# Six instead of three value blocks a layer moved onto chosen load engines, three of them fed by the Pool queue

## The chip, the core and the metric

The kernel runs on one core of a Trainium2 chip. The metric is the device time of one launch in microseconds (us), lower is better; the median of three runs before the change is 2574.92 us (2574.52 to 2575.61). All arithmetic is in float32.

## The reference

Two tokens (batch 2, one position, width 512) go twice through the same pair of layers: grouped attention over a cache of 32768 keys with 32 query heads on 8 key heads, and a gated feed-forward layer with a rectified gate.

```python
x = x + attention(layernorm(x), k_cache, v_cache, wq, wo)   # k, v: 2 x 8 x 32768 x 128
x = x + feed_forward(layernorm(x), W_gate, W_up, W_down)    # 512 -> 1792 -> 512
x = x + attention(layernorm(x), k_cache, v_cache, wq, wo)   # the same weights and caches again
x = x + feed_forward(layernorm(x), W_gate, W_up, W_down)
# attention: p = softmax(q k^T / sqrt(128)); out = (p v) reshaped @ wo
# feed_forward: gate = x W_gate; up = x W_up; (gate * (gate > 0) * up) @ W_down
```

The two caches hold 268 MB each and are read once a layer, but for a small part that the kernel keeps on the chip between its layers.

## The kernel before

A layer is 16 turns (`NG`), one for each pair of key head and batch entry. A turn needs the 32768 keys and the 32768 values of its pair, laid out by the host as 64 blocks of 128 partitions x 512 numbers (2 KB a partition). Half of them, 32 blocks (64 KB a partition, 8 MB), is one load. Eight blocks are a page.

SBUF holds one long tile, `arena`: three slots of 64 KB a partition, used in turn (`by_use`, `used`), and 29 KB beside them for small tiles (`ring`). Every big load is issued by SyncE (queue SP) in program order and waits there until its slot has been read out by TensorE. So the order of the loads is that of the code: in step `i` of a layer's loop come both halves of the keys of turn `i` (`keys`), then both halves of the values of turn `i-1` (`values`), and on TensorE the products with them in the same order. `k_tile` makes the scores of a page, `soft_max` the exponentials, `soft_tail` the transposed probabilities (VectorE, 32x32 blocks), `v_tile` adds the products with a page of values up in `acc`, `evacuate` scales `acc` into SBUF, `head_out` and `project` bring it through `wo`.

A load over 128 partitions gives each of the 16 load engines (the DMA engines) 8 partitions, that is 16 KB of each block. One group of blocks is treated apart. In turn `SIDE_TURN` the last `SIDE` = 3 blocks of page `SIDE_PAGE` are left out of the ordinary value load. The host has cut the 96 keys a row group that they hold into other rows (`side_blocks`, array `side`): two sets of 20 partitions, each with 20 KB a partition, whose source has 5 outer rows, so that 5 engines carry them. SP issues these two loads at the end of `values(SIDE_TURN)` and they take a slot of their own. Their products follow at once (`v_side`, 10 products over 64 partitions), with keys that `side_keys` made in `soft_tail` of that turn: three transposes of windows of the probabilities `p`, one memset on GpSimd, and one product with the mask `side_rows` that clears the unused rows.

Weights of the other stages go through the small tiles in pieces. At the end of layer 0 the next layer's first keys and part of its first values stay on the chip.

Of the kernel before, what the change touches and what calls it, by code (L numbers as in the profile page):

```python
# [46 lines left out]
C_SAME, C_MEAN, C_SEL, C_PAIR, C_SIDE, C_ONE, C_MHALF, C_END = 0, 128, 160, 192, 224, 225, 226, 228  # L47


@with_exitstack  # L50
def attention_reglu_decode(ctx: ExitStack, tc: tile.TileContext, x, k, v, wq, wo, wgu, wd, consts, side, out):
# [12 lines left out]
    def ring(at, width):  # L64
        if at < 0:
            assert at * KB + width <= 0 or (spill[0] + 1) * SLOT == RING
            at += (spill[0] + 1) * SLOT - RING
        at = int((RING + at) * KB)
        return arena[:, at : at + width]

    def slot(s, at=0, width=SLOT * KB):
        at = int((s * SLOT + at) * KB)
        return arena[:, at : at + width]

    def load(t, src):
        nc.sync.dma_start(t, src)
        return t
# [52 lines left out]
    selh = sel[:, :16]  # L130
    col = sel[:, :NB]
    pair = cst[:, C_PAIR : C_PAIR + 32]
    side_rows = cst[:, C_SIDE : C_SIDE + 1]
# [140 lines left out]

    def side_keys(p):
        W = SIDE_CHUNKS * 32
        t = ring(SIDE_KEYS_AT, 2 * W)
        at = SIDE_PAGE // 2 % 2 * D + (SIDE_PAGE % 2 * 8 + 8 - SIDE) * 32  # L280

        def windows(rows):
            return bass.AP(rows.tensor, rows.offset + at, [rows.ap[0], [SIDE_ROWS, SIDE_CHUNKS], [1, 32]])

        def chunks(rows):
            return rows.rearrange("p (k r) -> p k r", r=32)

        nc.gpsimd.memset(t[64:, W:], 0.0)
        nc.vector.transpose(chunks(t[:, :W]), windows(p))
        for c in (0, 32):  # L290
            nc.vector.transpose(chunks(t[c : c + 32, W:]), windows(p[64 + c : 96 + c]))
        nc.vector.tensor_scalar_mul(t, t, side_rows[:, 0:1])
        return t

    def v_side(L, n):
        s = by_use[0]
        vt = slot(s, 0, 2 * SIDE_CHUNKS * D)
        for c in range(2):
            load(vt[32 * c : 32 * c + SIDE_ROWS], side[L, c, :, : 8 * SIDE_CHUNKS * D].rearrange("e (r f) -> e r f", r=4))
        used(s)  # L300
        t, J = side_of.pop(n), SIDE_PAGE // 4
        for k in range(2 * SIDE_CHUNKS):
            nc.tensor.matmul(
                acc[32 * (k % 4) : 32 * (k % 4) + 16, :],
                t[:, 32 * k + 16 * J : 32 * k + 16 * J + 16],
                vt[:, k * D : (k + 1) * D],
                start=False, stop=k >= 2 * SIDE_CHUNKS - 4,
            )

    def v_tile(n, j, vt, first, last, blocks):  # L310
# [87 lines left out]
    for L in range(NLAYER):  # L398
# [3 lines left out]
        def keys(i):  # L402
            n = seq[i]
            if i < NG - 1:
                place_queries(i + 1, seq[i + 1])
            if L and i == 0:
                loads = list(kept_k)
                kept_k.clear()
            elif L and i == 1:
                f, g = key_slots  # L410
                loads = cuts(k, n, [(f, 0, 0, 8), (f, 16, 8, 16), (f, 32, 16, 32), (g, 0, 32, 48), (g, 32, 48, 64)])
            elif i == NG - 1:
                f, g = key_slots[:] = by_use[:2]
                loads = cuts(k, n, [(f, 0, 0, 32), (g, 0, 32, 48), (g, 32, 48, 64)])
            else:
                loads = whole(k, n)
            if not last and i == NG - 1:
                loads = list(loads)
                kept_k.extend(loads)
            for lo, _, t in by_page(loads):  # L420
                j = lo // 8
                k_tile(L, i, n, j, t)
                if L and i == 0:
                    yield
                if j == 1 and i >= 1:
                    soft_tail(L, i - 1, seq[i - 1])
                if j == 2 and i >= 2:
                    head_out(L, seq[i - 2])
                    if i % 2 == 1:
                        project((i - 3) // 2, load(ring(WO_AT, REP * D), wo[seq[i - 2] // NB]), False)  # L430
                    if i == NG - 1:
                        gather()

        def values(i, soft):
            n = seq[i]
            if i == NG - 1:
                if last:
# [108 lines left out]
```

## Time and profile before

| | |
|---|---|
| median of 3 runs (lowest to highest) | 2574.92 us (2574.52 to 2575.61) |
| the profiled execution's own time | 2574.12 us |
| its span, first to last instruction | 2572.3 us |
| TensorE busy with products | 51% of the span |
| VectorE busy | 6% |
| GpSimd busy | 6.7 us in 11 instructions |
| moved by DMA | 1105.95 MB in 29429 packets, mean 430 GB/s |
| share of the SP queue's packets of 16 engines' span | 99.7% |
| granted TensorE clock, mean | 0.75 |

The table is from the first three parts of the page and from the times. Busy times are sums over an engine's instructions; the share of a DMA queue is the time of its packets over 16 engines for the whole span, so 100% would mean that no load engine ever stood still. A view that cuts the span into stretches gives the same share for each of them: with 16 engines, one that stands still takes 0.06 off.

### The profile page before, as it was taken

Reading aid. Unit: us, or ns where it says so; the run is one execution under the profiler, and the core shown is the slowest. Engines: PE = TensorE matmul, PEld = TensorE weight load, DVE = VectorE, ACT = ScalarE, POOL = GpSimd, SP = SyncE. Lnnn points to the kernel's source line nnn. Section 1 sums busy time; section 2 is a strip of 40 time slices with the busy share of each in tenths; the row PEclk is TensorE's granted clock in tenths of the full one; section 3 lists DMA queues with packets and bytes.
Section 4 is the critical chain, followed back from the end, with each engine's and each line's share of the span. In section 5 each row is a group of like instructions: output and inputs, shape, how many; then the busy total and the mean of one; then the engine's idle time right before and its main releaser. Section 6 shows DMA issues by size and latency. Waiting matters only on the chain.

```text
span 2572.3 us, 19897 instructions
## 1 busy us (share of the span) xinstructions
PE 1304.3 (51%) x9452; PEld 342.7 (13%) x9452; DVE 153.0 (6%) x367; ACT 41.3 (2%) x69; POOL 6.7 (0%) x11
## 2 busy tenths in 40 slices
PE   2544454455445544555675554455445544554555
PEld 0111111111111111111121111111111111111112
DVE  0000000000000000000011000000000000000001
ACT  0000000000000000000000000000000000000000
POOL 0000000000000000000000000000000000000000
PEclk9777777777767777777887777777776777777788
DMA  9999999999999999999999999999999999999998
GB/s 425 430 432 438 431 432 431 435 429 437 427 435 436 426 437 430 436 431 421 422 412 434 436 430 433 435 432 434 430 438 426 436 434 430 437 428 433 431 435 376
DMA packets 29429, 1105.95 MB, mean 430 GB/s; under 512 B 3276, under 2 KB 3540, under 8 KB 6740
## 3 DMA queue, kind: packets, MB, share of 16 engines
q1 hardware_dynamic: 29188, 1104.56, 99.7%
q8 instruction: 74, 1.21, 0.2%
q10 hardware_dynamic: 160, 0.12, 0.0%
q14 instruction: 7, 0.06, 0.0%
HBM read 1104.60 MB, written 0.07 MB: 429 GB/s over the span
## 4 chain that ended last, share of the span: by engine, by line
DMA 67%; PE 24%; another core or an unknown queue 9%; DVE 0%; issue 0%; SPq 0%; ACTq 0%; POOL 0%; POOLq 0%; DVEq 0%
DMA arena<-k 46%; DMA arena<-v 16%; PE sc_odd L241 9%; PE sums L317 6%; PE sc_even L241 5%; DMA arena<-wo 2%; DMA cst<-consts 1%; DMA arena<-wd 1%; PE po L337 1%; PE sc_odd L210 1%; PE sums L241 1%; PE sums L348 1%; DMA arena<-wgu 1%; DMA arena<-wq 0%
## 5 line engine op out<-in xcount | busy, mean ns | idle before, releaser
L317 PE MATMUL sums<-arena 128*16 128x512 f32 (+1 forms) x4116 | 582.3, 717 | 600.7 <-DMA arena<-v 600.7
L241 PE MATMUL sc_odd<-arena,qz 128*32 128x512 f32 x2048 | 302.5, 745 | 293.6 <-DMA arena<-k 293.6
L241 PE MATMUL sc_even<-arena,qz 128*32 128x512 f32 x1920 | 277.5, 731 | 286.0 <-DMA arena<-k 286.0
L317 PEld LDWEIGHTS sums<-arena 128*16 128x16 f32 x4116 | 119.6, 109 | 1014.0 <-issue 519.6
L241 PEld LDWEIGHTS sc_odd<-arena,qz 128*32 128x32 f32 x2048 | 71.6, 133 | 504.6 <-DMA arena<-k 321.2
L241 PEld LDWEIGHTS sc_even<-arena,qz 128*32 128x32 f32 x1920 | 64.7, 131 | 473.2 <-DMA arena<-k 312.6
L331 DVE TENSOR_SCALAR arena<-sums,stat 128x512 f32<-128x512 f32 (+1 forms) x38 | 24.8, 665 | 779.4 <-PE sums L317 725.1
L266 DVE STREAM_TRANSPOSE arena<-arena 128x512 f32<-128x512 f32 x64 | 41.5, 687 | 2.5 <-ACT arena L259 2.5
L250 DVE TENSOR_REDUCE stat<-sc_odd 128x1 f32<-128x1024 f32 x16 | 19.6, 1225 | 339.7 <-PE sc_odd L241 339.7
L259 ACT ACTIVATE arena<-sc_odd,stat 128x1024 f32<-128x1024 f32 x16 | 17.8, 1114 | 1177.2 <-DVE stat L256 1177.2
L250 DVE TENSOR_REDUCE stat<-sc_even 128x1 f32<-128x1024 f32 x15 | 18.4, 1225 | 299.8 <-PE sc_even L241 299.8
L337 PE MATMUL po<-cst,arena 128*128 128x4 f32 x256 | 34.8, 259 | 1.8 <-DVE arena L331 1.8
L337 PEld LDWEIGHTS po<-cst,arena 128*128 128x128 f32 x256 | 32.0, 195 | 26.1 <-issue 23.5
L259 ACT ACTIVATE arena<-sc_even,stat 128x1024 f32<-128x1024 f32 x15 | 16.7, 1114 | 1069.9 <-DVE stat L256 1069.9
L272 DVE RECIPROCAL stat<-sm 128x1 f32<-128x1 f32 x32 | 5.3, 166 | 414.0 <-PE sm L270 414.0
L256 DVE TENSOR_REDUCE stat<-mp 128x1 f32<-128x32 f32 x32 | 6.1, 192 | 360.3 <-PE mp L254 360.3
L372 PE MATMUL sc_odd<-arena 128*32 128x224 f32 x256 | 19.7, 452 | 14.8 <-DMA arena<-wgu 13.5
L348 PE MATMUL sums<-arena,oT 128*2 128x512 f32 x112 | 15.4, 623 | 16.3 <-DMA arena<-wo 13.0
L210 PE MATMUL sc_odd<-arena 128*32 128x512 f32 x128 | 20.5, 733 | 5.6 <-DMA arena<-wq 3.1
L254 PEld LDWEIGHTS mp<-arena,cst 128*128 128x128 f32 x64 | 13.1, 257 | 52.4 <-issue 50.7
L162 PE MATMUL meana<-cst,stat 128*128 128x32 f32 x4 | 1.0, 342 | 35.5 <-DMA cst<-consts 35.0
L254 PE MATMUL mp<-arena,cst 128*128 128x32 f32 x64 | 17.0, 354 | 3.5 <-DVE arena L253 3.5
(70 smaller groups left out, 152.5 us busy)
## 6 DMA issues: line engine op xcount, KB each, us to landing
arena<-v SPq DMA_DIRECT2D x17, 2048.0 KB, 15.7
arena<-k SPq DMA_DIRECT2D x7, 4096.0 KB, 20.9
arena<-wo SPq DMA_DIRECT2D x16, 1024.0 KB, 50.9
arena<-v SPq DMA_DIRECT2D x2, 7424.0 KB
arena<-v SPq DMA_DIRECT2D x2, 4096.0 KB
arena<-wgu SPq DMA_DIRECT2D x8, 896.0 KB, 13.6
arena<-wgu SPq DMA_DIRECT2D x4, 1792.0 KB
arena<-wq SPq DMA_DIRECT2D x6, 1024.0 KB, 8.6
```

The costliest lines, as they stand in the source:

```text
L210: nc.tensor.matmul(qp[32 * c : 32 * c + 32, B, :], xT[:, kt, :], t[:, e * D : (e + 1) * D], start=kt == 0, stop=kt == KT - 1)
L241: nc.tensor.matmul(sc_of[n][32 * c : 32 * c + 32, B, :], qz[:, i % 2, 28 - 4 * j : 60 - 4 * j], kt[:, ch * D : (ch + 1) * D], start=j == 0 ...
L250: nc.vector.tensor_reduce(m1, sc_of[n], AX.XY, ALU.max)
L254: nc.tensor.matmul(mp[:, :32], same, mt, start=True, stop=True)
L256: nc.vector.tensor_reduce(nm, mp[:, :32], AX.X, ALU.max, negate=True)
L259: nc.scalar.activation(p, sc_of[n].rearrange("p a b -> p (a b)"), AF.Exp, bias=nm[:, 0:1], scale=1.0, accum_out=rs)
L266: nc.vector.transpose(pT[:, B * D : (B + 1) * D], p[:, B * D : (B + 1) * D])
L317: nc.tensor.matmul(acc[32 * c : 32 * c + 16, e * w : (e + 1) * w], pT[:, B, m, 16 * J : 16 * J + 16], vt[:, at * D + e * w : at * D + (e + ...
L331: nc.vector.tensor_scalar_mul(acs[:, at : at + w], acc[:, at : at + w], linv[:, 0:1])
L337: nc.tensor.matmul(po[:, :REP], acs[:, t * P : (t + 1) * P], selh[:, 4 * t : 4 * t + 4], start=t == 0, stop=t == 3)
L348: nc.tensor.matmul(op[32 * u : 32 * u + NB, :], oT[:, u, :], w[:, u * D : (u + 1) * D], start=pair_at == 0, stop=pair_at == HKV - 2)
L372: nc.tensor.matmul(gu[32 * j : 32 * j + 32, s, :], xT[:, at + e, :], t[:, f : f + HF], start=at + e == 0 and s == 0, stop=at + e == KT - 1 ...
```

## The change

`SIDE` goes from 3 to 6 blocks, `SIDE_TURN` from turn 13 to turn 11 of 16, and the rows of these blocks are cut anew:

- One SP load (`side`) brings 20 partitions of 48 KB, 5 outer rows, 12 packets of 16 KB for each of 5 engines; before it was two loads of 20 KB a partition, 8 packets of 20 KB for each of the five.
- Three loads of 4 partitions of 48 KB each (`alone`, to partitions 28, 64 and 92) are issued by GpSimd on the Pool queue. Their two access patterns have 4 and 3 outer rows. Ahead of the first and of the third go small loads of 4-byte elements (`turn_by`, into `turned`, which nothing reads), with 7 and 6 outer rows. The code counts on two things that the trace before cannot show, since its Pool queue carries nothing: that a load with 4 and 3 outer rows stays on one engine, and that the Pool queue deals its loads out to the engines in rotation. Then the small loads turn it on by 7 and by 6, and the three loads fall to engines 7, 8 and 15.
- The products (`v_side`, now 24 over 96 partitions) and the `evacuate` of that turn move from the end of `values(SIDE_TURN)` into `keys(SIDE_TURN + 2)`, after the second page of its first half. Until then the side blocks hold their slot.
- `side_keys` makes two key tiles `t` and `u` with eight transposes and four memsets, masks both and adds them.
[...]

```diff
-SCRATCH = 64
+SCRATCH = 512
-SIDE_TURN = NG - 3
-SIDE_PAGE, SIDE = 3, 3
-SIDE_WAYS, SIDE_ROWS, SIDE_CHUNKS, SIDE_GAP = 5, 20, 5, 64
+SIDE_TURN = NG - 5
+SIDE_PAGE, SIDE = 3, 6
+SIDE_WAYS, SIDE_ROWS, SIDE_CHUNKS, SIDE_GAP = 5, 20, 24, 64
+SIDE_END, ALONE, TURNED = 96, (28, 64, 92), (7, 0, 6)
...
     def side_keys(p):
...
-        nc.gpsimd.memset(t[64:, W:], 0.0)
-        nc.vector.transpose(chunks(t[:, :W]), windows(p))
-        for c in (0, 32):
-            nc.vector.transpose(chunks(t[c : c + 32, W:]), windows(p[64 + c : 96 + c]))
+        for g, c in enumerate((0, 1, 3)):
+            nc.vector.transpose(chunks(t, 0, 8 * g, 8), windows(c, 0, 20, 8))
+            nc.vector.transpose(chunks(u, 0, 8 * g, 8), windows(c, 132, 4, 8))
+        nc.vector.transpose(chunks(t, 2, 0, 24), windows(2, 0, 4, 24))
+        nc.vector.transpose(chunks(u, 2, 0, 24), windows(2, 68, 4, 24))
+        for c in (1, 3):
+            nc.gpsimd.memset(t[32 * c : 32 * c + 32], 0.0)
+            nc.gpsimd.memset(u[32 * c : 32 * c + 32], 0.0)
         nc.vector.tensor_scalar_mul(t, t, side_rows[:, 0:1])
+        nc.vector.scalar_tensor_tensor(t, u, side_rows[:, 1:2], t, ALU.mult, ALU.add)
...
-    def v_side(L, n):
+    def turn_by(n):
+        if n:
+            few = consts[: 5 * n, :1].rearrange("(e r) f -> e r f", r=5)[:, :4]
+            nc.gpsimd.dma_start(turned[: 4 * n, steps[0] : steps[0] + 1], few)
+        steps[0] += 1
+    def load_side(L, n):
         s = by_use[0]
-        vt = slot(s, 0, 2 * SIDE_CHUNKS * D)
-        for c in range(2):
-            load(vt[32 * c : 32 * c + SIDE_ROWS], side[L, c, :, : 8 * SIDE_CHUNKS * D].rearrange("e (r f) -> e r f", r=4))
+        vt = side_at[n] = slot(s, 0, 3 * SIDE_THIRD).rearrange("p (a f) -> p a f", a=3)[:, :, : SIDE_CHUNKS * D // 3]
+        load(vt[:SIDE_ROWS], side[L, :, : 4 * SIDE_CHUNKS * D])
+        part = 4 * SIDE_CHUNKS * D // 3
+        for e, (row, step) in enumerate(zip(ALONE, TURNED)):
+            turn_by(step)
+            nc.gpsimd.dma_start(vt[row : row + 4], alone[L, e, :, :part])
         used(s)
+    def v_side(n):
...
+                t[:SIDE_END, 32 * k + 16 * J : 32 * k + 16 * J + 16],
+                vt[:SIDE_END, k // 8, k % 8 * D : (k % 8 + 1) * D],
...
                 k_tile(L, i, n, j, t)
+                if j == 1 and i == SIDE_TURN + 2:
+                    v_side(seq[SIDE_TURN])
+                    evacuate(seq[SIDE_TURN], False)
...
             if i == SIDE_TURN:
-                v_side(L, n)
-            evacuate(n, i == NG - 1)
+                load_side(L, n)
+            else:
+                evacuate(n, i == NG - 1)
```

TensorE in layer 0 before, around the side products: L317 are products with values, L241 with keys, L303 those with the side blocks, `sm` belongs to `soft_tail`.

```order
L317 MATMUL sums<-arena 16x512 x8
L254 MATMUL mp_14_2285<-arena,cst 128x32
L317 MATMUL sums<-arena 16x512 x53
L303 MATMUL sums<-arena 16x512 x10
L241 MATMUL sc_odd<-arena,qz 32x512 x16
L270 MATMUL sm_14_2378<-stat,cst 128x1
```

The same engine after; L342, L244 and L328 are now the products with values, keys and side blocks, L362 is `head_out`.

```order
L257 MATMUL mp_12_1988<-arena,cst 128x32
L342 MATMUL sums<-arena 16x512 x16
L342 MATMUL sums<-arena 16x256 x4
L342 MATMUL sums<-arena 16x512 x32
L244 MATMUL sc_odd<-arena,qz 32x512 x16
L328 MATMUL sums<-arena 16x512 x24
L273 MATMUL sm_12_2097<-stat,cst 128x1
L244 MATMUL sc_odd<-arena,qz 32x512 x8
L362 MATMUL po_11_2108<-cst,arena 128x4 x4
```

The side products stood right behind the values of their turn; now they stand behind two pages of the next loaded keys, two turns earlier in the layer.

SyncE's queue in layer 0 after, around the side load, with what each load waits for (PE: its slot has been read; DMAHW and DMASW: earlier loads of the SP and ACT queues and of the Pool queue).

```order
L78 DMA arena<-v 128x13312 [waits DMAHW6_49,PE_49]
L78 DMA arena<-v 128x16384 [waits DMAHW7_49,PE_49]
L78 DMA arena<-side 20x3x4096 [waits DMAHW3_49,DMAHW0_49,PE_49]
L78 DMA arena<-k 128x16384 [waits DMAHW1_49,PE_49]
L78 DMA arena<-wo 128x2048
L78 DMA arena<-k 128x16384 [waits DMAHW2_49,PE_49]
L78 DMA arena<-v 128x16384 [waits DMASW4_49,DMASW2_49,DMAHW3_49,DMASW1_49,PE_49]
```

The last row is the next load into the slot that the side blocks hold: between the side load and it stand two loads of keys and `wo`, and its wait for TensorE is now the wait for the 24 side products.

GpSimd in layer 0 after, from the last of its four memsets on (L310 the turning loads, L322 the single-engine loads, L221 belongs to the queries of layer 1).

```order
L300 MEMSET arena 32x768
L310 DMA turned<-consts 28x1x1
L322 DMA arena<-alone 4x3x4096 [waits DMAHW0_49,PE_49]
L322 DMA arena<-alone 4x3x4096
L310 DMA turned<-consts 24x1x1
L322 DMA arena<-alone 4x3x4096
L221 TENSOR_TENSOR stat<-stat,cst 128x2 [waits DVE_49,Pool_49]
```

GpSimd, which issued no load before, now issues five in each layer; the first of the big ones waits until TensorE has read the slot out, and until layer 1 nothing but the other loads is queued behind it.

More of the change, by code (lines that the diff above doesn't have):

```diff
@@ L41, with attention_reglu_decode @@
 ENDING = (3, 2, 2, 1)
-SIDE_TURN = NG - 3
-SIDE_PAGE, SIDE = 3, 3
-SIDE_WAYS, SIDE_ROWS, SIDE_CHUNKS, SIDE_GAP = 5, 20, 5, 64
-C_SAME, C_MEAN, C_SEL, C_PAIR, C_SIDE, C_ONE, C_MHALF, C_END = 0, 128, 160, 192, 224, 225, 226, 228
+SIDE_TURN = NG - 5
+SIDE_PAGE, SIDE = 3, 6
+SIDE_WAYS, SIDE_ROWS, SIDE_CHUNKS, SIDE_GAP = 5, 20, 24, 64
+SIDE_END, ALONE, TURNED = 96, (28, 64, 92), (7, 0, 6)
+SIDE_THIRD = SIDE_CHUNKS * D // 3 + 16
+C_SAME, C_MEAN, C_SEL, C_PAIR, C_SIDE, C_ONE, C_MHALF, C_END = 0, 128, 160, 192, 224, 226, 227, 229
 @with_exitstack
-def attention_reglu_decode(ctx: ExitStack, tc: tile.TileContext, x, k, v, wq, wo, wgu, wd, consts, side, out):
+def attention_reglu_decode(ctx: ExitStack, tc: tile.TileContext, x, k, v, wq, wo, wgu, wd, consts, side, alone, out):
     nc = tc.nc
@@ L132, in attention_reglu_decode @@
     pair = cst[:, C_PAIR : C_PAIR + 32]
-    side_rows = cst[:, C_SIDE : C_SIDE + 1]
+    side_rows = cst[:, C_SIDE : C_SIDE + 2]
+    turned = sb.tile([4 * max(TURNED), NLAYER * len(TURNED)], F32, name="turned")
     mhalf = cst[:, C_MHALF : C_MHALF + NB]
@@ L278, in side_keys @@
         W = SIDE_CHUNKS * 32
-        t = ring(SIDE_KEYS_AT, 2 * W)
+        t, u = (ring(SIDE_KEYS_AT + e * W / KB, W) for e in range(2))
         at = SIDE_PAGE // 2 % 2 * D + (SIDE_PAGE % 2 * 8 + 8 - SIDE) * 32
[L282 to L286, printed above, removed]
-        nc.gpsimd.memset(t[64:, W:], 0.0)
-        nc.vector.transpose(chunks(t[:, :W]), windows(p))
@@ L290, in side_keys, with windows, chunks @@
-        for c in (0, 32):
-            nc.vector.transpose(chunks(t[c : c + 32, W:]), windows(p[64 + c : 96 + c]))
+        def windows(c, start, step, n):
+            rows = p[32 * c : 32 * c + 32]
+            return bass.AP(rows.tensor, rows.offset + at + start, [rows.ap[0], [step, n], [1, 32]])
+        def chunks(t, c, lo, n):
+            return t[32 * c : 32 * c + 32, 32 * lo : 32 * (lo + n)].rearrange("p (k r) -> p k r", r=32)
+        for g, c in enumerate((0, 1, 3)):
+            nc.vector.transpose(chunks(t, 0, 8 * g, 8), windows(c, 0, 20, 8))
+            nc.vector.transpose(chunks(u, 0, 8 * g, 8), windows(c, 132, 4, 8))
@@ L300, in v_side @@
+    steps, side_at = [0], {}
+    def load_side(L, n):
+        s = by_use[0]
+        vt = side_at[n] = slot(s, 0, 3 * SIDE_THIRD).rearrange("p (a f) -> p a f", a=3)[:, :, : SIDE_CHUNKS * D // 3]
[4 more added lines that the diff above has]
+            nc.gpsimd.dma_start(vt[row : row + 4], alone[L, e, :, :part])
         used(s)
-        t, J = side_of.pop(n), SIDE_PAGE // 4
@@ L302, in v_side @@
-        for k in range(2 * SIDE_CHUNKS):
+    def v_side(n):
+        vt, t, J = side_at.pop(n), side_of.pop(n), SIDE_PAGE // 4
+        for k in range(SIDE_CHUNKS):
             nc.tensor.matmul(
                 acc[32 * (k % 4) : 32 * (k % 4) + 16, :],
-                t[:, 32 * k + 16 * J : 32 * k + 16 * J + 16],
-                vt[:, k * D : (k + 1) * D],
-                start=False, stop=k >= 2 * SIDE_CHUNKS - 4,
+                t[:SIDE_END, 32 * k + 16 * J : 32 * k + 16 * J + 16],
+                vt[:SIDE_END, k // 8, k % 8 * D : (k % 8 + 1) * D],
+                start=False, stop=k >= SIDE_CHUNKS - 4,
@@ L501 @@
     cst[:, C_PAIR : C_PAIR + 32] = np.equal.outer(rows // 4, np.arange(32))
-    cst[:, C_SIDE] = (rows < 64) & (rows % 32 < SIDE_ROWS)
+    cst[:, C_SIDE] = (rows < SIDE_ROWS) | (rows // 4 == 16)
+    cst[:, C_SIDE + 1] = (rows // 4 == 7) | (rows // 4 == 23)
     cst[:, C_ONE] = 1.0 / D
@@ L512, in side_blocks @@
     def side_blocks(v):
-        W = 2 * SIDE_CHUNKS * D
-        sets = np.zeros((NLAYER, 2, SIDE_WAYS, 4 * W + SIDE_GAP), np.float32)
+        W = SIDE_CHUNKS * D
+        side = np.zeros((NLAYER, SIDE_WAYS, 4 * W + SIDE_GAP), np.float32)
+        alone = np.zeros((NLAYER, len(ALONE), 3, 4 * W // 3 + SIDE_GAP), np.float32)
         for L in range(NLAYER):
@@ L518, in side_blocks @@
             keys = v[n, SIDE_PAGE // HALF, :, hi - SIDE * D : hi].reshape(4, 32, SIDE, D).transpose(0, 2, 1, 3)
-            rows = np.zeros((4, SIDE_CHUNKS * SIDE_ROWS, D), np.float32)
-            rows[:, : 32 * SIDE] = keys.reshape(4, 32 * SIDE, D)
-            rows = rows.reshape(2, 2, SIDE_CHUNKS, SIDE_ROWS, D).transpose(1, 3, 0, 2, 4)
-            sets[L, ..., : 4 * W] = rows.reshape(2, SIDE_WAYS, 4 * W)
-        return sets
+            keys = keys.reshape(4, 32 * SIDE, D)
+            low = keys[[0, 1, 3]]
+            side[L, :, : 4 * W] = low[:, :160].reshape(3, 8, SIDE_ROWS, D).transpose(2, 0, 1, 3).reshape(SIDE_WAYS, 4 * W)
+            fours = (low[:, 160:], keys[2, :96], keys[2, 96:])
+            for e, rows in enumerate(fours):
+                rows = rows.reshape(SIDE_CHUNKS, 4, D).transpose(1, 0, 2)
+                alone[L, e, :, : 4 * W // 3] = rows.reshape(3, 4 * W // 3)
+        return side, alone
     wq = con(a["A_wq"].reshape(D, 2, HKV * REP // 2, 4, 32).transpose(0, 1, 3, 2, 4)).reshape(D, -1)
@@ L536 @@
     }
-    arrays["side"] = side_blocks(arrays["v"])
+    arrays["side"], arrays["alone"] = side_blocks(arrays["v"])
     nc = bacc.Bacc("TRN2", target_bir_lowering=False, num_devices=1, dynamic_dma_scratch_size=SCRATCH)
```

## Prediction

> **What bounds the kernel now.** I read the page from its top, then the chain that ended last, then the span cut into stretches at the end of each layer, then single groups for prices. From the page:
>
> ```profile
> span 2572.3 us, 19897 instructions
> PE 1304.3 (51%) x9452; PEld 342.7 (13%) x9452; DVE 153.0 (6%) x367; ACT 41.3 (2%) x69; POOL 6.7 (0%) x11
> DMA packets 29429, 1105.95 MB, mean 430 GB/s; under 512 B 3276, under 2 KB 3540, under 8 KB 6740
> q1 hardware_dynamic: 29188, 1104.56, 99.7%
> q8 instruction: 74, 1.21, 0.2%
> q10 hardware_dynamic: 160, 0.12, 0.0%
> DMA 67%; PE 24%; another core or an unknown queue 9%; DVE 0%; issue 0%; SPq 0%; ACTq 0%; POOL 0%; POOLq 0%; DVEq 0%
> ```
>
> TensorE works half of the span, the load engines all of it, and the chain is mostly DMA. So the kernel lasts as long as its latest load engine needs; what the others do beside it is free. The question is how uneven the 16 are. In the stretches (the last two columns are the DMA share and GB/s) it can be counted, 0.0625 for each engine:
>
> ```profile
> 1219.00:1224.00 5.00, 5.00 (x47) 1.33 (x43) 1.66 (x3) 1.21 (x2) 0.00 (x0) 1.00 0.86 354
> 2563.00:2564.00 1.00, 1.00 (x24) 1.00 (x20) 0.90 (x5) 0.00 (x0) 0.00 (x0) 0.50 0.79 330
> 2566.50:2567.00 0.50, 0.00 (x0) 0.00 (x0) 0.00 (x0) 0.00 (x0) 0.00 (x0) 1.00 0.50 197
> 2567.00:2567.50 0.50, 0.34 (x13) 0.37 (x17) 0.00 (x0) 0.00 (x0) 0.00 (x0) 1.00 0.36 143
> 2568.00:2568.50 0.50, 0.40 (x19) 0.16 (x11) 0.00 (x0) 0.00 (x0) 0.00 (x0) 1.00 0.24 74
> 2568.50:2569.00 0.50, 0.50 (x19) 0.24 (x11) 0.00 (x0) 0.00 (x0) 0.00 (x0) 1.00 0.00 0
> 2561.20:2566.60 5.40, 4.35 (x74) 2.96 (x66) 1.50 (x7) 0.36 (x1) 0.00 (x0) 0.68 0.82 336
> ```
>
> At the end of the launch three engines are done by 2561.2 (0.79 to 0.82 is 13 of 16), eight by 2566.7, ten by 2567.2, and about four work until 2568.5. At the end of layer 0 (1219 to 1224) two to three stand still again. So three engines have 5 to 7 us to spare in each layer while the latest set the pace. That the pace is theirs in both places shows in the chain, here at the end of layer 0 and at the end of the launch (start, length, what):
>
> ```profile
> 1228.92 17.57 DMA arena<-v
> 1269.87 18.50 DMA arena<-wo
> 1288.51 1.12 PE sums L181 x32
> 2543.06 25.24 DMA arena<-wd
> 2568.34 1.11 PE tot L181 x24
> 2569.48 0.35 DVE x L185
> ```
>
> Why they are uneven: the 74 instruction packets took 0.2% of 16 x 2572.3 us, or 82 us, 1.1 us each (0.8 to 1.4 by the rounding). Dealt evenly they would cost each engine 5 us. The records of single landings, which no view lists, show that they are not: before the side loads of each layer eight engines land within 1.5 us of the first, the other eight 4.7 to 6.7 us behind it, growing in steps of 1.5 us at the times of those packets. The side loads of before charge five of the early eight; three early ones are left, those that stand still above.
>
> **The change, part by part.** *Bytes.* A full load takes 19.35 us, the distance of two waits for values that ended with a landing:
>
> ```profile
> 1069.61 3.61 PE L317 MATMUL sums<-arena 128*16 128x512 f32 x16 [9.37 <-DMA arena<-v]
> 1088.96 9.39 PE L317 MATMUL sums<-arena 128*16 128x512 f32 x64 [10.11 <-DMA arena<-v]
> ```
>
> It is 32 blocks, so a block (16 KB an engine) costs each engine 0.605 us. Per layer, against a plain load of all blocks, before and after:
>
> - the eight late engines: 3 blocks less (-1.81 us), now 6 less (-3.63): they gain 1.81 us;
> - engines 0 to 4: 160 KB side rows less 48 KB, now 192 less 96: they gain 16 KB, 0.6 us;
> - the three idle ones: 48 KB less, now 96 more: they lose 9 blocks, 5.45 us.
>
> The three then end at 2561.2 + 5.45 = 2566.7, ahead of today's last 2568.4. If one of the last four is of the five, a layer gains 0.6 us, if none is, up to 1.7 (2568.4 less 2566.7). By the landing records the last is a late engine, 7.9 us behind the first, and the latest of the five is 7.2 behind; the change makes that 7.9 - 1.8 = 6.1 and 7.2 - 0.6 = 6.6, so the gain is 7.9 - 6.6 = 1.3 us. At the end of layer 0 the same records have 2.5 us for the last late engine, 1.8 for the last of the five: 1.8 - 0.6 = 1.2, again 1.3 us. That layer's chain is DMA up to 1288.37, so it counts too. I take 1.3 for each layer, between the ends 0.6 and 1.7.
>
> *The slot held longer.* Issue to landing of a big load and the products of the side blocks:
>
> ```profile
> arena<-v SPq DMA_DIRECT2D x55, 48.3
> 1028.44 5.51 PE L241 MATMUL sc_odd<-arena,qz 128*32 128x512 f32 x32 [10.99 <-DMA arena<-k]
> 1173.57 2.74 PE L303 MATMUL sums<-arena 128*16 128x512 f32 x20
> SPq L76 <- PE sums L303: 3.4, 3, 2.1
> ```
>
> A load is issued 48.3 us ahead of its landing and needs 19.35 itself: 29 us of other loads lie ahead of it. The slot of the side blocks is now free only after two pages of keys (5.51 us) and 24 side products (48 instructions of 2.74/20 us, 6.6 us), 12.4 us with the issue, behind a landing, and ahead of the next load into it lies only one half of keys, 19.35 us. The latest engine has 7 us to spare, one that leads it by 4 us (the widest spread left after the side loads) still 3. The wait of SP costs nothing; behind it on SP stand only loads that land later. TensorE itself has pauses of 9 to 11 us ahead of each half (the waits above), which cover 14 more products, some 4 us. `head_out` of the turn now follows its `evacuate` closely, with a page of keys between.
>
> *VectorE and GpSimd.*
>
> ```profile
> L289 DVE STREAM_TRANSPOSE arena<-arena 128x160 f32<-128x160 f32 x1 | 0.3, 303 | 0.0
> L291 DVE STREAM_TRANSPOSE arena<-arena 32x160 f32<-32x160 f32 x2 | 0.7, 336 | 0.0
> L266 DVE STREAM_TRANSPOSE arena<-arena 128x512 f32<-128x512 f32 x4 | 2.6, 687 | 0.0
> L292 DVE TENSOR_SCALAR arena<-arena,cst 128x320 f32<-128x320 f32 x1 | 0.4, 386 | 0.1
> L272 DVE RECIPROCAL stat<-sm 128x1 f32<-128x1 f32 x1 | 0.2, 168 | 13.3 <-PE sm L270 13.3
> L138 POOL MEMSET arena<- x1: 4364/4364/4364, 1.0 to 1.0; 128x5120 f32 x1
> ```
>
> From 160 to 512 columns a transpose grows by 0.35 us, 1.0 ns a column: six of 256 columns at 0.43 us and two of 768 at 0.94, and two passes over 768 columns at about 0.85 each, 6.2 us instead of 1.4. They fall into the 13.3 us in which VectorE waits for `sm`. Four memsets at 768/5120 of 4.36 us are 2.6 us on an idle GpSimd. The mask's column, `SCRATCH` and the 52 elements of 4 bytes of the turning loads a layer I set at 0: the ACT queue's 160 packets show 0.0% of the engines.
>
> *Packets of the Pool queue.* No trace here has one. Between SP's packets of 64 KB there go 12 of 16 KB on each of the three engines. Below, they cost their bytes, 0.605 us each, as in the sum; above, as much as an instruction packet of the same 16 KB, 1.1 us. [...] They are issued when a slot comes free, with some 29 us of SP's loads still ahead, and the three engines lead at that time: no one waits for them.
>
> **Sum.** 2 x 1.3 = 2.6 us: 2574.1 of the profiled execution becomes 2571.5. The median lies 0.8 above it, so 2574.9 becomes 2572.3. That is 0.1%, half of the 0.2% (5.1 us) that a measurement of this kernel can tell from no change. A bound from above: the stretches from 2561.2 to 2568.5 hold about 2.3 us of idle time per engine, so perfect balance would bring no more than that there, and about as much in layer 0.
>
> **Rivals.** *No gain at all:* one of the five is the last in both layers and a step of 1.5 us falls on it, or the turn order shifts the instruction packets. Two times 0.6 us or less: 2573.7 to 2576. For it: the five end within 0.7 us of the last.
>
> *Slower, the Pool packets cost more than their bytes.* Place: the three engines. With 1.1 us a packet, 12 x 0.5 = 6 us more, they end at 2566.7 + 6 = 2572.7, 4.3 behind today's last, and nothing later in the layer evens that out: +8.6 us, 2583.5. It decides from 1.7 us on, 0.14 us a packet; from 0.36 a packet it would be measurable. For it: the instruction row; against it: the ACT row.
>
> *Slower, the bytes go to other engines.* If the three loads fall to late engines, those lose 9 blocks against now, 5.45 us: an average one, done at 2567.2, ends at 2572.7, +4.3 a layer, 2583.5. If each load deals its 4 partitions to engines 0 to 3, these get 240 KB instead of 112, +4.8 us: 7.2 + 4.8 = 12.0 against 7.9, +4.1 a layer, 2583.1. [...]
>
> *Engines run dry at the held slot:* the side products would have to end 7 us later than worked out, then 1 us more for each further one. I see nothing that would do it.
>
> *Clearly faster:* over 5.1 us would need more than perfect balance gives.
>
> **How the numbers follow.** The forecast (2571 to 2574) has 0.57, no gain 0.20, dear Pool packets 0.08, other engines 0.09, a dry slot 0.02, clearly faster 0.04. The first two lie within 0.2%, and so would the cheap half of the dear packets: same 0.78, slower 0.18, faster 0.04. The range takes in the first two and the low ends of the slower ones: 2569.5 to 2579.5, which leaves out the 0.17 of full price above and a little below.
>
> **What would show it.** In the last 10 us the DMA share stays near 1.0 until about 2565 and then falls within 2 us, instead of standing at 0.8 for 5 us. Near the end of layer 0 the dip to 0.86 is gone or shallower. The wait for `wd` ends 2 to 3 us earlier. A Pool queue appears with 36 packets of 16 KB a layer, about 0.6 us each. If the dear packets were right, three engines would work alone at the end, share 0.19; if the bytes went elsewhere, 1 to 4 engines would, with others still idle early. VectorE's waits for `sm` and `po` should not grow, nor SP's for the side products beyond some us.

## The result and the profile after

The changed kernel takes 2597.39 us, median of four runs (2594.80 to 2598.69), beside 2574.72 for the kernel before, also in four runs (2574.33 to 2575.61). The ratio is 1.0086, 95% interval 1.0069 to 1.0104: some 22.5 us slower, where 2.6 us less had been forecast, and far above the range. The profiled execution took 2594.80 us. From its page:

```profile
span 2593.0 us, 20044 instructions
PE 1306.7 (50%) x9504; PEld 346.3 (13%) x9504; DVE 162.6 (6%) x379; ACT 41.3 (2%) x69; POOL 18.5 (1%) x27
GB/s 422 435 436 425 437 429 435 433 428 435 435 433 433 424 439 427 363 423 429 425 420 434 435 434 430 431 434 426 440 430 432 436 433 428 433 357 436 428 440 373
q1 hardware_dynamic: 29218, 1103.31, 98.8%
q0 software_dynamic: 1376, 1.19, 0.1%
L328 PE MATMUL sums<-arena 96*16 96x512 f32 x96 | 15.2, 799 | 31.3 <-DMA arena<-alone 16.3
```

The same GB/s line of the kernel before:

```profile
GB/s 425 430 432 438 431 432 431 435 429 437 427 435 436 426 437 430 436 431 421 422 412 434 436 430 433 435 432 434 430 438 426 436 434 430 437 428 433 431 435 376
```

TensorE's work and the bytes are nearly what they were; the SP queue's share fell from 99.7% to 98.8%, and 0.9% of 2593 us is 23 us, about the whole loss. It is lost at two places: of the 40 slices two that were full before, the 17th (363 GB/s) and the 36th (357), are the side stretches of the two layers. The last line of the first block says what for: TensorE stood still ahead of the side products, for a single-engine load (`alone`).

Here is TensorE around the side products of layer 0 (start, length, engine, operation, and in brackets the idle time ahead and what ended it):

```profile
1027.18 4.99 PE L244 MATMUL sc_odd<-arena,qz 128*32 128x512 f32 x32 [12.62 <-DMA arena<-k]
1048.43 8.01 PE L328 MATMUL sums<-arena 96*16 96x512 f32 x48 [16.26 <-DMA arena<-alone]
1079.41 3.61 PE L342 MATMUL sums<-arena 128*16 128x512 f32 x16 [9.95 <-DMA arena<-v]
```

The two pages of keys are done at 1032.2, the side rows are there at 1048.4. The other engines in the same stretch, GpSimd and then SyncE:

```profile
979.27 1.33 POOL L322 DMA_DIRECT2D arena<-alone  x2 [934.48 <-PE sc_even L244]
980.59 0.59 POOL L310 DMA_DIRECT2D turned<-consts  x1
1018.88 0.66 POOL L322 DMA_DIRECT2D arena<-alone  x1 [37.70 <-issue]
```

```profile
978.98 0.94 SPq L78 DMA_DIRECT2D arena<-side  x1
993.88 0.35 SPq L78 DMA_DIRECT2D arena<-k  x1
994.28 0.42 SPq L78 DMA_DIRECT2D arena<-wo  x1
1014.62 0.33 SPq L78 DMA_DIRECT2D arena<-k  x1
1056.49 6.49 SPq L78 DMA_DIRECT2D arena<-v  x2
```

SP's next load into the slot goes out at 1056.49, the moment the side products end; what it had issued before (the last at 1014.62) is used up by then. The chain of waits runs the same way, `alone`, side products, next values:

```profile
1018.88 29.30 DMA arena<-alone
1048.18 0.24 issue
1048.43 8.01 PE sums L328 x48
1056.43 0.06 PE sm L273
1056.49 22.87 DMA arena<-v
```

And the stretches show the load engines running dry (last two columns: DMA share and GB/s):

```profile
1040.00:1044.00 4.00, 0.00 (x0) 0.00 (x0) 0.00 (x0) 0.00 (x0) 0.00 (x0) 0.50 1.01 434
1044.00:1048.00 4.00, 0.00 (x0) 0.00 (x0) 0.00 (x0) 0.00 (x0) 0.00 (x0) 0.50 0.41 172
1048.00:1052.00 4.00, 3.57 (x20) 0.93 (x24) 0.00 (x0) 0.00 (x0) 0.00 (x0) 0.50 0.00 0
1052.00:1058.00 6.00, 6.00 (x52) 1.56 (x42) 1.50 (x3) 0.00 (x0) 0.00 (x0) 0.85 0.42 142
1058.00:1062.00 4.00, 3.75 (x39) 1.61 (x35) 0.68 (x3) 0.00 (x0) 0.00 (x0) 1.00 0.72 311
```

The missing shares are 2.4 + 4.0 + 3.5 + 1.1 = 11 us per engine. Layer 1 has the same kind of hole at 2308 to 2326, 10 us by the same sum. The two holes make 21 us, and the profiled execution is 20.7 us longer than that of before (2594.8 against 2574.1).

Why the loads are late is in the records of single packets, which no view lists. In layer 0 the Pool queue's packets of 16 KB took 0.61 us each, as forecast. But as long as SP's packets have 64 KB, each comes 3.03 us behind the one before on its engine: one packet of SP (2.42 us) stands between the two. And a load on one engine is not on one engine alone: of the 1376 packets 72 are the data (16 KB), the other 1304 have 4 or 16 bytes. Each of the three loads puts 12 small packets on each engine that it gives no data, and one more on all 16; a turning load puts 2 on each. The first turning load of a layer waits for nothing and has passed long before (its 32 packets at 49 to 53 us in layer 0). So in the side stretch an engine passes 13 + 13 + 2 + 13 = 41 packets of that queue, and if each waits for one of SP's, that is 41 packets of SP. The data packets by their starts:

```
first load     984.1 ... 1015.0   12 packets, 3.03 us apart but for one pair
second load   1013.2 ... 1027.3   the last nine 0.9 us apart, beside the 8-KB packets of wo
third load    1028.3 ... 1047.1   six 3.03 us apart, the last six with nothing of SP beside them
```

### The profile page after: what moved, and what is told of

Its sections match the earlier page's. It is cut to its first block, busy times and chain, and to the rows that moved or that the text cites. A ratio compares the mean times of both kernels' runs of the same rounds, so it can differ in the third digit from the quotient of the medians.

```text
span 2593.0 us, 20044 instructions
## 1 busy us (share of the span) xinstructions
PE 1306.7 (50%) x9504; PEld 346.3 (13%) x9504; DVE 162.6 (6%) x379; ACT 41.3 (2%) x69; POOL 18.5 (1%) x27
## 3 DMA queue, kind: packets, MB, share of 16 engines
q1 hardware_dynamic: 29218, 1103.31, 98.8%
q0 software_dynamic: 1376, 1.19, 0.1%
## 4 chain that ended last, share of the span: by engine, by line
DMA 66%; PE 23%; another core or an unknown queue 8%; issue 2%; DVE 0%; SPq 0%; POOL 0%; ACTq 0%; POOLq 0%; DVEq 0%
DMA arena<-k 47%; DMA arena<-v 12%; PE sc_odd L244 8%; PE sums L342 6%; PE sc_even L244 6%; DMA arena<-wo 2%; DMA arena<-wd 1%; DMA cst<-consts 1%; DMA arena<-alone 1%; PE sums L328 1%; PE sc_odd L213 1%; DMA arena<-wgu 1%; PE po L362 1%; PE sums L244 1%
## 5 line engine op out<-in xcount | busy, mean ns | idle before, releaser
L342 PE MATMUL sums<-arena 128*16 128x512 f32 (+1 forms) x4112 | 582.9, 719 | 599.9 <-DMA arena<-v 599.9
L244 PE MATMUL sc_odd<-arena,qz 128*32 128x512 f32 x2048 | 296.4, 733 | 281.6 <-DMA arena<-k 281.6
L244 PE MATMUL sc_even<-arena,qz 128*32 128x512 f32 x1920 | 276.8, 729 | 285.4 <-DMA arena<-k 285.4
L342 PEld LDWEIGHTS sums<-arena 128*16 128x16 f32 x4112 | 119.4, 109 | 1015.5 <-issue 515.8
L244 PEld LDWEIGHTS sc_odd<-arena,qz 128*32 128x32 f32 x2048 | 71.2, 132 | 487.4 <-DMA arena<-k 308.0
L244 PEld LDWEIGHTS sc_even<-arena,qz 128*32 128x32 f32 x1920 | 64.2, 130 | 472.6 <-DMA arena<-k 311.9
L362 PE MATMUL po<-cst,arena 128*128 128x4 f32 x256 | 34.0, 256 | 2.1 <-DVE arena L356 2.1
L362 PEld LDWEIGHTS po<-cst,arena 128*128 128x128 f32 x256 | 31.2, 191 | 26.3 <-issue 21.8
L328 PE MATMUL sums<-arena 96*16 96x512 f32 x96 | 15.2, 799 | 31.3 <-DMA arena<-alone 16.3
```

What stands on the lines that cost most here:

```text
L244: nc.tensor.matmul(sc_of[n][32 * c : 32 * c + 32, B, :], qz[:, i % 2, 28 - 4 * j : 60 - 4 * j], kt[:, ch * D : (ch + 1) * D], start=j == 0 ...
L328: nc.tensor.matmul(acc[32 * (k % 4) : 32 * (k % 4) + 16, :], t[:SIDE_END, 32 * k + 16 * J : 32 * k + 16 * J + 16], vt[:SIDE_END, k // 8, k ...
L342: nc.tensor.matmul(acc[32 * c : 32 * c + 16, e * w : (e + 1) * w], pT[:, B, m, 16 * J : 16 * J + 16], vt[:, at * D + e * w : at * D + (e + ...
L362: nc.tensor.matmul(po[:, :REP], acs[:, t * P : (t + 1) * P], selh[:, 4 * t : 4 * t + 4], start=t == 0, stop=t == 3)
```

## The experiments

In the edited kernels line numbers are up to two higher. The theories that the expectations name (some of them with the first turning load still in the count): DRAIN is what was just said, the Pool queue gets one packet past for each of SP's. RING: the third load was issued 37.7 us late (the wait above that ends on no one) for want of room in `SCRATCH` (the program's `dynamic_dma_scratch_size`), and that is what made it late. OTHER: the rest of the change (more work of VectorE and GpSimd, products two turns later) costs the time.

**More room in `SCRATCH`.**

```diff
-SLOT, RING, ARENA = 64, 192, 221
-SCRATCH = 512
+SLOT, RING, ARENA = 64, 192, 220.5
+SCRATCH = 1024
...
```

> SCRATCH 1024 instead of 512 (the place for it is won by moving two small tiles). Theory DRAIN (a packet of the Pool queue gets one turn after each 64 KB packet of SP's queue, 2.4 us, and each single-engine load puts 13 packets on all 16 engines, so the three loads pass one after the other): the third load is issued at once, within 5 us of the second turning load, but still lands some 65 to 70 us after the first was issued, and the time stays at 2590 to 2599 us. Theory RING (the loss is the 37.7 us that GpSimd stands ahead of the third load, because its descriptors do not fit): the third load lands some 36 us after its issue, before the products want it, and the time falls to 2571 to 2576 us.

Measured: 2601.15 us, ratio 1.0102 (1.0081 to 1.0122). GpSimd and TensorE in layer 0:

```profile
981.24 0.66 POOL L322 DMA_DIRECT2D arena<-alone  x1
```

```profile
1048.40 8.04 PE L328 MATMUL sums<-arena 96*16 96x512 f32 x48 [16.23 <-DMA arena<-alone]
```

The third load now goes out at once, 37.6 us earlier, and its rows come at the same time to 0.03 us. The wait is gone with the larger `SCRATCH` (what did not fit into the smaller one no trace shows), and without it the loss is as large (whether these two runs are slower than the changed kernel, 2601 against 2597, the overlapping intervals do not tell). RING falls.

**No Pool loads.** In `load_side` the loop over `ALONE` does nothing, so the kernel leaves out the rows of three engines.

> The five Pool-queue loads of each layer are left out; the side products run on what the slot held, so that the data of engines 7, 8 and 15 are missing. All else of the change stays (key tiles, late products, SP's side load). DRAIN and RING: the dry stretch after the side products is gone and the time is 2569.5 to 2573.5 us, below the kernel before, since the late engines carry 12 blocks less in all. Theory OTHER (the longer chain on VectorE and GpSimd, or the slot held for longer, costs the time): 2585 us or more.

Measured: 2571.97 us, ratio 0.9989 (0.9980 to 0.9998). The hole is gone, with all other parts of the change in place; the same two stretches:

```profile
1044.00:1048.00 4.00, 0.00 (x0) 0.00 (x0) 0.00 (x0) 0.00 (x0) 0.00 (x0) 1.00 1.05 446
1048.00:1052.00 4.00, 3.33 (x20) 0.91 (x24) 0.00 (x0) 0.00 (x0) 0.00 (x0) 0.57 1.06 459
```

OTHER falls. The 2.8 us below the kernel before are no gain of the balance: 1.25 MB less are loaded than before, 2.9 us at the 433.3 GB/s that 16 engines move with 64 KB in 2.42 us.

**Smaller packets of SP.** The two halves of the values of the side turn and of the keys two turns later are loaded in pieces of 8 blocks: SP's packets are 16 KB instead of 64.

```diff
...
-            yield from cuts(src, n, [(by_use[0], 0, lo, hi)])
+            s = by_use[0]
+            yield from cuts(src, n, [(s, 2 * (a - lo), a, min(a + step, hi)) for a in range(lo, hi, step)])
...
```

> Values of turn 11 and keys of turn 13 in loads of 8 blocks, so that SP's packets beside the Pool loads are 16 KB instead of 64 KB; the rest as in the changed kernel. DRAIN: a Pool packet waits 0.6 us instead of 2.4, the third load lands 25 to 40 us after the first was issued, and the time falls to 2570 to 2577 us. A fixed latency of the Pool queue of some 13 to 35 us a load: no change, 2590 to 2599 us. RING: its wait of 37.7 us shrinks likewise, so this run does not part it from DRAIN.

Measured: 2575.08 us, ratio 1.0002 (0.9993 to 1.0012). TensorE comes to the side products without a wait, and the data packets of the Pool queue now stand 1.2 us apart on their engine, and the last starts at 1014.8 instead of 1047.1:

```profile
1021.51 5.73 PE L329 MATMUL sums<-arena 96*16 96x512 f32 x48
```

The Pool loads are the same, byte for byte and packet for packet; only what they take turns with has changed. That is what DRAIN says and RING does not: by the first run here, the wait for room moves no landing.

**Two Pool loads instead of three.** Engines 7 and 8 by one load, 15 and 0 to 4 by another, which takes over SP's part; rows of 48 KB, 4 packets an engine.

```diff
...
-SIDE_END, ALONE, TURNED = 96, (28, 64, 92), (7, 0, 6)
+SIDE_END, SIDE_AT, PAIR_AT, TURNED = 96, 8, 88, (7, 6, 2, 6)
...
+        nc.gpsimd.dma_start(vt[PAIR_AT : PAIR_AT + 8], alone[L, :, :W].rearrange("e (r a f) -> e r a f", r=4, a=SIDE_PIECES))
+        turn_by(TURNED[2 * L + 1])
+        nc.gpsimd.dma_start(vt[SIDE_AT : SIDE_AT + 24], side[L, :, :W].rearrange("e (r a f) -> e r a f", r=4, a=SIDE_PIECES))
...
```

> Two Pool loads in place of three and of SP's side load: 8 partitions for engines 7 and 8 and 24 partitions for engines 15 and 0 to 4, the same bytes on each engine, in 4 packets of 48 KB an engine instead of 12 of 16 KB (partitions 88 to 95 and 8 to 31). DRAIN: 14 packets an engine (2 + 5 + 2 + 5) instead of 43, landed some 40 us after the issue, ahead of the side products; no dry stretch; 2570.5 to 2574 us with the gain forecast for the balance. RING: no wait for room either (14 packets), the same. If the price lies in loads of the Pool queue as such, 2580 us or more.

Measured: 2610.20 us, ratio 1.0141 (1.0126 to 1.0156), a miss. The Pool packets of 48 KB took 3.5 us in layer 0 (median) instead of the 1.8 of their bytes, and SP's of 64 KB, from the first of them to the last, 3.4, up to 5.05. So SP's own loads came late; the second half of the values, at 1005.6 before this edit:

```profile
1022.33 8.48 PE L343 MATMUL sums<-arena 128*16 128x512 f32 x64 [26.35 <-DMA arena<-v]
```

**The same with packets of 16 KB** (`SIDE_PIECES` 3 instead of 1), to tell the size of the packets from the number of engines.

> The previous kernel (two Pool loads, 48-KB packets) with the rows cut in three: the same two Pool loads, on two and on six engines, now 12 packets of 16 KB for each engine. DRAIN (the Pool queue passes one packet an engine for each packet of SP, and every load has as many packets on all 16 engines): 30 packets an engine instead of 43; the first load is through at about 1015, the second at 1030 to 1036 in layer 0, at or a little behind the time at which the side products are wanted (1032). The dry stretch is gone or under 3 us a layer: 2572 to 2580. LARGE PACKETS were what made the previous one slow: the same, and SP's packets of 64 KB take 2.4 us again. SIX ENGINES (a Pool load over six engines is itself what slows SP, whatever the packets' size): again over 2600.

Measured: 2607.38 us, ratio 1.0125 (1.0111 to 1.0139). Only SIX ENGINES had that. A Pool packet of 16 KB took 1.04 us instead of 0.61, SP's of 64 KB beside them 3.0 instead of 2.42. The stretches of this kernel show it as engines that are busy and move little:

```profile
1000.00:1020.00 20.00, 8.58 (x64) 1.84 (x64) 0.00 (x0) 0.00 (x0) 0.00 (x0) 0.65 1.02 355
1020.00:1040.00 20.00, 0.69 (x4) 0.20 (x8) 0.00 (x0) 0.00 (x0) 0.00 (x0) 0.61 0.97 252
```

DRAIN's count held in both kernels: from the first Pool packet to the last with data an engine passes on average 13 and 29 SP packets, those of 4 bytes included, beside 5 + 2 + 4 = 11 and 13 + 2 + 12 = 27 of the Pool queue. What it had wrong is the price of a packet. Pool loads with data on two and six engines are dearer here than their bytes; with data on one they are not. Why was not tried; the two edits also move the rows to other partitions and SP's side load into the Pool queue.

**One Pool load of the three.** The loop over `ALONE` ends after the first; a second turning load in layer 1 keeps the rotation.

> Only the first single-engine load (engine 7) is left in each layer; the loads for engines 8 and 15 and the second turning load are left out, so these rows of the side blocks are not there. DRAIN: 2 + 13 packets an engine, landed by about 1016 in layer 0, nothing waits for it and no engine runs dry: 2571 to 2575, near the kernel without any Pool load (2572.0). EACH LOAD COSTS (a Pool load costs SP's packets something while it is under way, and three of them add up to the loss): a third of 25 us, about 2580.

Measured: 2572.02 us, ratio 0.9989 (0.9980 to 0.9997); the last data packet starts at 1014.8, nothing waits for it. As DRAIN had it. 0.85 MB less are loaded than before, 2.0 us of the 2.4. In layer 0 of this kernel the packets can be followed engine by engine, since each starts within 6 ns of the end of the one before: all 16 engines pass 13 packets of the Pool queue with 12 of SP between them, one by one in turn, whether the Pool packet has 16 KB or 4 bytes.

**Only one half load cut:** the first half of the later keys, with packets of 16 KB.

```diff
...
+            s, size = by_use[0], BLOCKS if lo and not late else step
...
+                loads = whole(k, n, 0, 8 if i == SIDE_TURN + 2 else BLOCKS)
...
```

> Of the four half loads around the side loads only one is cut into packets of 16 KB: the first half of the keys of the turn two later, 1008 to 1027 in layer 0. DRAIN: the first Pool load is through at about 1015, the second at 1027, the third between 1033 and 1043; the dry stretch shrinks from 11 us a layer to 0 to 3. Time 2573 to 2580, and if it is gone, 0 to 1.5 us faster than with all four halves cut (2575.1), since only a quarter of the SP packets are small. If the time that the third load takes is not set by the number of SP packets beside it, the loss stays: over 2590.

Measured: 2573.73 us, ratio 0.9996 (0.9987 to 1.0005). The third load's last data packet starts at 1023.7, some ten microseconds ahead of what I had worked out, so the times by load in the expectation were wrong; there is no hole.

**The cuts alone:** all four halves cut, no Pool loads.

> The kernel without the five Pool loads (their rows of the side blocks are left out), with the four half loads around the side load cut into packets of 16 KB. It asks where the gain of the better balance went in the kernel with cut SP loads and all Pool loads (2575.1, against 2572.0 without both). SMALL SP PACKETS cost it: 0.005 us more for each 16 KB (0.612 against 2.43 / 4) over some 120 packets an engine is 0.6 us a layer, and up to 1.3 if gaps between them count too: 2573.2 to 2574.6. POOL PACKETS cost it: 2572.0 as without the cuts.

Measured: 2573.66 us, ratio 0.9998 (0.9989 to 1.0006), against 0.9989 without the cuts: that is 2.8 us under the kernel before without the cuts and 0.7 with them. The intervals overlap, so the times alone do not show it. The stretches do, in one execution each: by the bytes moved from 960 to 1100 and from 2230 to 2370, against 433.3 GB/s, the engines lose 1.2 and 1.1 us with the cuts and 0.3 and 0.4 without. So SMALL SP PACKETS cost some 0.8 us a layer.

**The same half in packets of 32 KB** (16 instead of 8 blocks).

> As the kernel with only the first half of the later keys cut, but into packets of 32 KB instead of 16. DRAIN: beside packets of 32 KB the Pool packets come some 1.8 us apart (1.2 + 0.6); the third load is through between 1028 and 1040 in layer 0 instead of 1024, still ahead of 1046, when SP's loads run out. No dry stretch, and half as many small packets: 2572.5 to 2574.5, the same as with 16 KB (2573.7) or up to 0.5 us less. If SP's packets had to be as small as those of the Pool queue for the loads to pass, the third load ends after 1046 and the time is over 2580.

Measured: 2589.09 us, ratio 1.0058 (1.0045 to 1.0070), a miss. TensorE, SyncE and two of the stretches:

```profile
1043.72 7.28 PE L329 MATMUL sums<-arena 96*16 96x512 f32 x48 [21.15 <-DMA arena<-alone]
```

```profile
1051.06 6.50 SPq L78 DMA_DIRECT2D arena<-v  x2
```

```profile
1044.00:1048.00 4.00, 4.00 (x24) 0.89 (x20) 0.00 (x0) 0.00 (x0) 0.00 (x0) 0.54 0.38 164
1048.00:1052.00 4.00, 4.00 (x38) 1.18 (x34) 0.93 (x2) 0.00 (x0) 0.00 (x0) 1.00 0.00 0
```

The last data packet started at 1040.0, the upper end of what was expected, and I had compared that with the wrong time: the engines run dry at about 1045, but by then the 48 side products (7.3 us) must be over, so the rows must be there by 1038. Each microsecond behind that is a microsecond of the hole: landed 5.7 behind it, the hole is 6.3 us (the bytes moved from 1040 to 1060, against 433.3 GB/s).

**Another half in packets of 16 KB:** the second half of the side turn's values, 984 to 1003.

```diff
...
+            s, size = by_use[0], step if lo else BLOCKS
...
+                pieces = whole(v, n, SIDE if i == SIDE_TURN else 0, 8 if i == SIDE_TURN else BLOCKS)
...
```

> Again one half load of the four is cut into packets of 16 KB, but the earliest one that can matter: the second half of the values of the side turn, 984 to 1003 in layer 0, when the first Pool load begins to pass. DRAIN counts SP's packets beside each load: the first Pool load is through at about 1003 instead of 1015, but then the second meets SP packets of 64 KB again and gets through only with the 8-KB packets of wo (1018 to 1030), and the third needs 12 packets at 3.03 us with nothing small beside it, so it ends between 1040 and 1050 as in the changed kernel. The dry stretch stays: 2590 to 2600. SMALL PACKETS ANYWHERE (the loads gain what the first one gains, 12 us): the third ends at about 1035, no dry stretch, 2573 to 2576.

Measured: 2573.52 us, ratio 0.9998 (0.9988 to 1.0007). The time is that of SMALL PACKETS ANYWHERE, and the load was earlier still: the last data packet starts at 1026.5, not 1035. My count had been wrong in one point: I had the three loads pass one after another. They stand side by side. The engine of the third load does not wait for the data on the other two; it has only its own small packets ahead, 13 + 13 + 2 = 28, and these pass at one for each of its own SP packets, 0.61 us each while those have 16 KB. In the changed kernel the two readings look alike, because a small packet costs 2.42 us of waiting there and one with data 3.03.

**The test of that:** only the first 16 blocks of that half in packets of 16 KB, the rest in packets of 32 KB.

```diff
...
+            ends = [lo, *range(lo + size, lo + 17, size), hi] if size < BLOCKS else [lo, hi]
+            yield from cuts(src, n, [(s, 2 * (a - lo), a, b) for a, b in zip(ends, ends[1:])])
...
```

> The second half of the side turn's values again, but only its first 16 blocks in loads with packets of 16 KB, the other 16 blocks as one load with packets of 32 KB. PER ENGINE (the rows of the three loads stand side by side: each engine passes one packet of the Pool queue for each SP packet that it carries itself, so the engine of the third load has 28 four-byte packets to pass before its 12 of 16 KB, while the other two engines are already at their own): 16 + 8 SP packets until 1003 in layer 0, 4 to 7 of the keys until 1015, so the third load's data begin at about 1012; three or four go beside the 64-KB keys, the rest beside the 8-KB packets of wo, and the last starts between 1024 and 1032. No dry stretch, 2572.5 to 2575, since 24 small packets an engine cost no more than the 32 of the last kernel. SERIAL (a load's data begin when those of the load ahead are through, as it looked in the changed kernel): first load through at about 995, second at 1020 to 1026, third at 1040 to 1050, a dry stretch of 5 to 12 us a layer, 2585 to 2600.

Measured: 2573.89 us, ratio 0.9998 (0.9989 to 1.0007). The last data packet starts at 1028.0, inside the 1024 to 1032 of PER ENGINE; SERIAL falls. TensorE waits 1.61 us for the rows, which is early enough:

```profile
1033.78 5.35 PE L330 MATMUL sums<-arena 96*16 96x512 f32 x48 [1.61 <-DMA arena<-alone]
```

A rough count over the kernels with all three loads fits: from the first Pool packet to the last with data an engine passes, on average, the side rows left out and SP's 4-byte packets included, 41 SP packets (keys in packets of 32 KB) and 42 (first 16 blocks), beside the 40 Pool packets that the engine of the third load has up to its last data. In the changed kernel it is 35.5, and then SP has none left: the last six packets pass alone, 0.6 us apart. In the three kernels with a whole half or more in packets of 16 KB the average is higher, 47 to 55; why was not followed up (it also counts engines whose Pool packets are through earlier).

## Why the prediction was wrong, point by point

**What bounds the kernel** held, also the reason given for it: by the landing records of before, eight engines fall back one after another in steps of some 1.5 us (the latest is 1.8 us behind the first at 100 us, 3.4 at 530, 6.5 at 1158), and the other eight stay within 1.3 us of the first. And the change's loads went where they were meant to: 36 packets of 16 KB a layer on the Pool queue, each load's data on one engine. The rival that they go elsewhere did not come. No trace names the engines, but the last landings of the launch, below, show that the three loads fell to the three early ones. That 4 and 3 outer rows keep a load's data on one engine is what the 72 packets of these six loads show: never two of a load's 12 at a time.

**Bytes.** The mechanism was right: the change makes the 16 engines end together. By the records of single landings, the 16 of the launch's last load lie 7.9 us apart before, 8.5 without Pool loads, 8.2 with one of them (two engines are still far ahead), and 3.2, 2.2 and 2.6 with all three and one half load of SP cut (keys, values, first 16 blocks). The size of the gain can be read only where the holes are gone, and it is not shown to be what was forecast. The dips are filled too. One more stretch of before, and then the kernel with the values cut, in this stretch and three that the prediction showed of before (0.86, 0.36 and 0.24):

```profile
2561.20:2565.00 3.80, 3.80 (x62) 2.69 (x58) 1.50 (x7) 0.36 (x1) 0.00 (x0) 0.55 0.83 345
```

```profile
1219.00:1224.00 5.00, 5.00 (x49) 1.35 (x45) 1.66 (x3) 1.21 (x2) 0.00 (x0) 1.00 1.01 419
2561.20:2565.00 3.80, 1.94 (x56) 1.44 (x56) 1.35 (x7) 0.00 (x0) 0.00 (x0) 1.00 0.99 408
2567.00:2567.50 0.50, 0.50 (x16) 0.34 (x16) 0.00 (x0) 0.00 (x0) 0.00 (x0) 1.00 0.01 4
2568.00:2568.50 0.50, 0.03 (x4) 0.00 (x0) 0.36 (x2) 0.00 (x0) 0.00 (x0) 1.00 0.00 0
```

What each stretch loses, from the bytes moved in it against 433.3 GB/s, in us:

```
                           before   keys cut   values cut   first 16 blocks cut
960 to 1100 (side rows)      0.2       0.9        0.9               0.8
1200 to 1340 (layer end)     5.8       5.6        4.9               4.3
2230 to 2370 (side rows)     0.2       0.9        0.9               0.8
2500 to the end              7.3       7.0        5.9               6.6
```

With the values and the first 16 blocks cut, the balance brings 0.7 to 1.5 us at the end of a layer, some 2.2 in all, against 1.3 a layer forecast; with the keys cut it is 0.5 in all. These are single executions, and those of the kernel before lie up to 3.4 us apart, so the size stays open. The side stretches take 1.1 to 1.3 back, for the Pool loads and SP's small packets together. The medians lie 0.7, 1.1 and 0.8 us under those of before (keys, values, first 16 blocks); each interval includes 1, so that the kernel became faster at all is not shown.

**Packets of the Pool queue** is where the prediction failed: "They are issued when a slot comes free, with some 29 us of SP's loads still ahead, and the three engines lead at that time: no one waits for them." One did wait: the rows landed at 1048.2, 16 us after the products could have begun, and the load engines stood still for 11 us in this layer and 10 in the other. I had priced what the packets cost the engine (0.605 us, measured 0.61; the rival of dear packets did not come) and not how long the queue takes to get them through. Half of the working was within reach: 12 packets, each behind one of 2.42 us, take 12 x 3.03 = 36 us, more than the 29. I had read the 64 KB in the packets of SP and left it. But the 36 us alone would have done no harm: with one load the last data packet starts at 1014.8, long before 1032. It took the 28 small packets ahead of the third load's data as well, and no trace of before has such packets. I had no reading of how a second queue gets past SP's packets of 64 KB; that its packets cost their bytes and no waiting was my estimate. The runs show turns: the 3.03 us from one data packet to the next are 2.42 + 0.61, a packet of SP and one of the Pool queue; each row of 16 KB took a turn of its own, and so did each 4-byte packet (with one load, 13 Pool packets with 12 of SP between them on all 16 engines).

**The turning loads** I set at nothing "the 52 elements of 4 bytes": their bytes cost next to nothing (a small packet of that queue took 9 ns, median), but one of the two loads is 2 of the 41 turns of an engine. The same goes for the small packets of the other loads, of which I knew nothing.

**The slot held longer.** The 12.4 us for pages, products and issue were about right (5.0 and 8.0 us in this trace), and so were the 7 us to spare and the price of the rival that engines run dry at the slot: "7 us later than worked out, then 1 us more for each further one". It forecast the slot free at 1027.2 + 12.4 = 1039.6; it was free at 1056.5, 16.9 later, which by that rule is a hole of 9.9 us, and 11 were measured in that layer. I gave this case 0.02 with "I see nothing that would do it": the only thing looked at was TensorE, whereas the side products also wait for a load that no trace had shown.

**VectorE and GpSimd** were sized right and mattered nowhere: VectorE 4.8 us more a layer (162.6 against 153.0 in all), as worked out; the four memsets of a layer took 3.0 us instead of 2.6.

**The chances** do not add up as written: the first two and half of the dear packets' 0.08 make 0.81 for the same time and leave 0.15 for slower, where 0.78 and 0.18 stand.

## What to carry to other kernels

For a load that goes in a second queue beside large packets, count its packets, not its bytes: in these runs it got one turn an engine for each packet of the other queue (3.03 us from one data packet to the next, 2.42 of them the other queue's packet of 64 KB), so it lasted as many of those as it had packets, and loads on one engine put small packets on the 15 others too. Work out the landing time that way, and compare it with the time at which the data must be there for everything that holds on to the slot to be over. If it is too late, smaller packets in the other queue for only as long as the load needs (here 24 instead of 8 on each engine) let it through at a cost of under 1 us a layer. And a better balance of the engines brought at most some 2 us here, too little for these runs to show.

## What the runs showed that I had not expected

- A load from GpSimd on one engine puts as many small packets as it has data packets, 12, and one more on each of the other 15: with the turning loads 1304 of 1376 packets of the Pool queue.
- With 512 bytes of scratch the issue of the third load stood 37.7 us with no releaser in the trace; with 1024 it did not. It changed no landing.
- Pool loads on two and six engines slowed everything: 16 KB took 1.04 us instead of 0.61, SP's 64 KB 3.0 instead of 2.42, and the engines read 0.97 busy at 252 GB/s. On one engine at a time there was no such loss. The share of busy time alone would have hidden it.
- Cutting SP's packets from 64 to 16 KB costs little but not nothing: 0.614 us each (median beside the side rows) instead of a quarter of 2.42, and some 0.8 us a layer for four half loads.
